# Projecting part of x inside the first ten steps of an attention loop, and reading the output weights in eight parts

## The chip, the cores and the metric

The kernel runs on one core of a Trainium2 chip. The metric is device time in microseconds (us). Before the change the median of three runs is 1559.05 us (1558.44 to 1567.2).

A core has five engines that run side by side, each through its own list of instructions in order: PE (TensorE: matrix multiplies and transposes into PSUM), DVE (VectorE: elementwise work and reductions), ACT (ScalarE: activations and copies), POOL (GpSimd) and SP (SyncE, which here only issues DMAs). They wait for each other on semaphores. DMA transfers are moved by 16 DMA engines that all issuing queues share.

## The reference

One transformer block with adaptive layer norm: 2048 tokens of width D = 640, H = 32 heads of 128 with cached keys and values of 2048 positions, then a small shift mixer and an MLP.

```python
x = A_x
mod = (silu(c) @ w_mod).reshape(1, 6, 1, 640)
sa, ca, ga, sb, cb, gb = (mod[:, i] for i in range(6))
h = layernorm(x) * (1 + ca) + sa
q = (h @ wq) split into 32 heads of 128
p = softmax(q @ k_cache^T * 128 ** -0.5)
x = x + ga * ((p @ v_cache), heads side by side) @ wo
h = layernorm(x) * (1 + cb) + sb
x = x + gb * mixer_and_mlp(h, w1, w2, w3, w4)
```

## The kernel before

**Planning.** The code isn't a list of instructions per engine; it calls `G.op(engine, fn, r=..., w=...)` and `G.dma(...)` with the keys that an operation reads and writes. `Prog` (line 20) derives the semaphore waits from the keys, and each engine runs its operations in the order of these calls. So where a call stands decides what it is behind on its engine. DMAs on "sync" stand in SP's queue in the same way.

**Prologue (lines 329 to 445).** SP issues, in this order: x block 0 (512 rows, 640 KB), c, x block 1, the first third of w_mod (1600 KB, the columns for sa and ca), x blocks 2 and 3, wq and the transposed K and V of head 0, the rest of w_mod (3200 KB), wq and K of head 1, and the whole of wo (5120 KB, line 353). c is turned to columns by its DMA and goes through Silu (363, 364); `cols` (371) multiplies it with w_mod, and ACT writes shift and 1 + scale to mcol (430, 431). Each block cc of x is then taken through four functions: `stats` (bn_stats and bn_aggr on DVE, 384 and 387, and a Sqrt on ACT, 389), `normed` (reciprocal, 393, and (x - mean) * rstd, 396, on DVE), `to_hT` (for each of KT = 5 column blocks: four PE transposes, 407, and an eviction that applies shift and scale, three on ACT, 411, and two on DVE, 416), and `q_head0` (five matmuls with head 0's wq, 250, and an ACT copy to QT, 257). All four blocks are done, but for the last `q_head0`, before the loop. The prologue's scratch (x, w_mod, statistics, the identity) lies in `ring`, the buffer that the loop uses for probabilities.

**Loop (line 558).** A step s handles one tile of 128 queries of one head: 16 tiles a head, NG = 512 in all. PE multiplies Q with K (`qk`, lines 301 and 15) into PSUM in two halves; DVE scales and negates each half into negS and takes its minimum (604); POOL joins the two minima (609); ACT takes the exponential of the 2048 columns to bf16 in Pb (612). The probabilities have to be transposed for the product with V. For tiles 3 and 10 of even heads and 2, 3 and 10 of odd ones (PE_STEPS) PE does it (267) and ACT copies (274); for all others SP issues a DMA transpose from Pb to PTs, mostly two tiles at once (235). `pv` (317) multiplies with V nine steps later (PVD = 9); ring has RP = 10 slots. ACT copies the result to Of every second tile (591), POOL normalizes it (461 to 468) and sends it to DRAM (475). Between these, PE projects the queries of the next head piece by piece (`q_piece`), and SP reads the next wq, K and V.

Steps 0 to 2 also hold `mod_rows` (447): for the other four parts of the modulation, broadcast to all partitions, 25 matmuls and 5 ACT copies (456); step 3 adds 1 to one part (566). Step 0 holds the last `q_head0`. wo is first used when the output projection begins (546), behind the loop.

**Behind the loop** come the output projection, the second layer norm, the mixer and the MLP (lines 642 to 886).

Of the kernel before, what the change touches and what calls it, by code (L numbers as in the profile page):

```python
# [7 lines left out]
ACT = mybir.ActivationFunctionType  # L8
BF16 = mybir.dt.bfloat16
F32 = mybir.dt.float32  # L10
# [113 lines left out]
def bass_adaLN_cond__mha_block_cached__mixer_s_mlp__prompt_kernel(  # L124
# [21 lines left out]
    with ExitStack() as es:  # L146
# [9 lines left out]
        if True:  # L156
            with ExitStack() as es1:
# [32 lines left out]
                XO = SK  # L190
                x_sb = flat[:, XO:XO + NQT * D].rearrange("p (t d) -> p t d", t=NQT)
                WO_ = 6 * SK
                wmod = flat[:, WO_:WO_ + KT * 2 * D].rearrange("p (k n) -> p k n", k=KT)
                RO = 13 * SK
                wmodr = flat[:, RO:RO + KT * 4 * D].rearrange("p (k n) -> p k n", k=KT)
                BO = RO + KT * 4 * D
                s_bc = flat[:, BO:BO + KT * 128].rearrange("p (k q) -> p k q", k=KT)
                ones_f = flat[:, BO + KT * 128:BO + KT * 128 + 256].bitcast(F32)
                SO = BO + KT * 128 + 256
                st = flat[:, SO:SO + NQT * 24].bitcast(F32).rearrange("p (t z) -> p t z", t=NQT)  # L200
                CO = SO + NQT * 24
                c_f = flat[:, CO:CO + 2 * KT].bitcast(F32)
                mcol = flat[:, CO + 2 * KT:CO + 6 * KT].bitcast(F32)
                c_sb = flat[:, CO + 6 * KT:CO + 7 * KT]
                s_col = flat[:, CO + 7 * KT:CO + 8 * KT]
                IO = CO + 8 * KT
                ident = flat[:, IO:IO + 128]
                assert IO + 128 <= 2 * RP * SK and XO + NQT * D <= WO_ and WO_ + KT * 2 * D <= 10 * SK
# [115 lines left out]
                WMK = ringk(WO_, WO_ + KT * 2 * D)  # L324
                WRK = ringk(RO, 2 * RP * SK)
                XK = [ringk(XO + cc * 4 * D, XO + (cc + 1) * 4 * D) for cc in range(NQC)]

                def load_x(cc):
                    G.dma("sync", lambda e: e.dma_start(
                        x_sb[:, 4 * cc:4 * cc + 4], x2d[cc * 512:(cc + 1) * 512, :].rearrange("(t p) d -> p t d", p=128)),  # L330
                        ("x", cc), w=[("x", cc)])

                def load_mod(part, dst, n0, n1):
                    G.dma("sync", lambda e: e.dma_start(
                        dst, w_mod[:, n0:n1].rearrange("(k p) n -> p k n", p=128)), ("wm", part), w=[("wm", part)])

                def load_c(e):
                    with nc.allow_non_contiguous_dma(reason="tiny c vector"):
                        return e.dma_start(c_sb, c[0].rearrange("(kt p) -> p kt", p=128))
# [15 lines left out]
                G.op("gpsimd", lambda g: g.memset(ident, 0.0), w=["id0"])  # L355
                G.op("gpsimd", lambda g: g.memset(ones_f, 1.0), w=["onesf"])
                G.op("gpsimd", lambda g: g.affine_select(out=ident, in_=ident, pattern=[[-1, 128]],
                                                         compare_op=ALU.not_equal, fill=1.0, base=0, channel_multiplier=1),
                     r=["id0"], w=["ident"])
                G.op("gpsimd", lambda g: g.tensor_copy(identf[:], ident), r=["ident"] + ringk(IO, IO + 128), w=["identf"])  # L360
                G.op("gpsimd", lambda g: g.memset(Vaug[:, :, :, 1:2], 1.0), w=["ones"])
                G.op("gpsimd", lambda g: g.memset(Vaug[:, :, :, 258:259], 1.0), w=["ones1"])
                G.op("scalar", lambda a: a.activation(s_col, c_sb, ACT.Silu), r=["c"], w=["scol"])
                G.op("scalar", lambda a: a.activation(c_f, c_sb, ACT.Silu), r=["c"], w=["cf"])
                for k in range(KT):
                    G.op("gpsimd", lambda g, k=k: g.tensor_scalar(out=s_bc[:, k, :], in0=ones_f, scalar1=c_f[:, k:k + 1],
                                                                  scalar2=1.0, op0=ALU.mult, op1=ALU.mult),
                         r=["onesf", "cf"] + WRK, w=[("sbc", k)])

                def cols(t):  # L370
# [7 lines left out]
                    PTp[:, b * 1024:b * 1024 + 512] for b in range(2)]  # L378
                TK = [("Sb", 0), ("Sb", 1), ("Sb", 2), ("Sb", 3), ("O", 0), ("O", 1)]

                def stats(cc):
                    for t in range(4 * cc, 4 * cc + 4):
                        for z in range(2):
                            G.op("vector", lambda v, t=t, z=z: v.bn_stats(st[:, t, 6 * z:6 * z + 6], x_sb[:, t, z * HD:(z + 1) * HD]),  # L384
                                 r=[("x", cc)], w=[("st", t, z)])
                    for t in range(4 * cc, 4 * cc + 4):
                        G.op("vector", lambda v, t=t: v.bn_aggr(mv[:, t, :], st[:, t, :]),
                             r=[("st", t, 0), ("st", t, 1)] + WRK, w=[("mv", t)])
# [526 lines left out]
```

## Time and profile before

| what | value |
|---|---|
| median of 3 runs | 1559.05 us |
| profiled execution's own time | 1558.54 us |
| its span | 1556.4 us |
| granted clock of TensorE, mean | 0.997 |
| PE, DVE, ACT, POOL busy | 94%, 88%, 81%, 42% of the span |
| first L604 (DVE, tile 0) | 36.16 us |
| first exponential (ACT, tile 0) | 39.78 us |
| exponential of tile 10 | 66.56 us |
| last exponential | 1238.0 us |

Times in the profile count from the span's start. Rows of the timeline give start, time taken, engine, line and operation, with the idle time before it and what ended it in brackets. Several instructions in one row are merged. SP's rows are DMA issues: their time is what SP needed to hand the transfer over, not the transfer. A row of waits reads "who waited <- for whom: us in total, times, longest". A row of the windows table gives a stretch, its length, each engine's busy time with its number of instructions, the granted clock, the mean share of the 16 DMA engines (over 1 when packets overlap on an engine) and the rate moved.

### The profile page before, as it was taken

The numbers are of one execution on the slowest core, as the hardware profiler recorded it, in microseconds if no ns is written. First come the engines' busy times: TensorE is split into PE (matmuls) and PEld (weight loads), VectorE is DVE, ScalarE is ACT, GpSimd is POOL, SyncE is SP. The second block draws the span as 40 slices with busy tenths as digits, with TensorE's granted clock in tenths as the row PEclk, the third lists the DMA queues.
The fourth block names the chain that finished last, engine by engine and source line by source line (L and its number), as shares of the span: only waits on it lengthen the run. The fifth ranks groups of instructions, "written<-read, shape, count | busy, mean of one in ns | idle before, by whom it ended". The sixth has DMA issues, their size and how long they took to land.

```text
span 1556.4 us, 32631 instructions
## 1 busy us (share of the span) xinstructions
PE 1463.7 (94%) x13446; PEld 899.4 (58%) x12663; DVE 1375.9 (88%) x2431; ACT 1259.2 (81%) x1177; POOL 647.4 (42%) x1526
## 2 busy tenths in 40 slices
PE   4899999998999999999999999999999899999999
PEld 2466556565656665656566656666565665554545
DVE  6999999999999999999999999999999737667425
ACT  4999999999999999999999999999999800034230
POOL 0145444444445444445444545444454533323100
PEclk9999999999999999999999999999999999999999
DMA  9999999999999999999999999999999998825100
GB/s 300 235 218 227 243 232 229 235 236 239 233 241 239 233 240 234 242 235 226 248 234 240 236 233 244 245 238 226 235 243 234 239 251 184 156 56 140 35 22 35
DMA packets 1123416, 330.32 MB, mean 212 GB/s; under 512 B 1071104, under 2 KB 1117248, under 8 KB 1123264
## 3 DMA queue, kind: packets, MB, share of 16 engines
q1 hardware_dynamic: 1114784, 307.10, 98.6%
q0 software_dynamic: 6144, 16.79, 3.7%
q10 hardware_dynamic: 2336, 4.34, 0.8%
q8 instruction: 104, 1.70, 0.4%
q14 instruction: 48, 0.39, 0.1%
HBM read 43.48 MB, written 19.40 MB: 40 GB/s over the span
## 4 chain that ended last, share of the span: by engine, by line
ACT 54%; PE 21%; DMA 11%; DVE 10%; issue 3%; POOL 1%; SPq 0%; DVEq 0%
ACT ring L612 44%; DMA ring<-ring 10%; PE Sps L546 9%; DVE negS L604 8%; PE Sps L852 4%; ACT ring L274 3%; ACT kv L257 3%; ACT Of L591 3%; PE Oaug L803 2%; PE QPp L803 2%; PE PTp L317 1%; PE Sps L788 1%; DVE ring L384 1%; DMA kv<-Of 0%; PE Oaug L725 0%
## 5 line engine op out<-in xcount | busy, mean ns | idle before, releaser
L604 DVE TENSOR_SCALAR_CACHE_REDUCE negS<-Sps 128x1024 f32<-128x1024 f32 x1024 | 1176.1, 1221 | 26.7 <-PE Sps L15 26.1
L612 ACT ACTIVATE ring<-negS,small 128x2048 bf16<-128x2048 f32 x512 | 1034.9, 2054 | 15.5 <-POOL small L609 14.5
L317 PEld LDWEIGHTS PTp<-kv,ring 128*128 128x128 bf16 x8192 | 546.9, 97 | 351.2 <-issue 89.5
L317 PE MATMUL PTp<-kv,ring 128*128 128x129 bf16 x8192 | 636.4, 221 | 40.5 <-DMA ring<-ring 39.6
L15 PE MATMUL Sps<-kv 128*128 128x512 bf16 x1009 | 382.7, 379 | 9.9 <-DVE negS L604 5.9
L609 POOL TENSOR_SCALAR small<-small 128x1 f32<-128x1 f32 x512 | 145.8, 285 | 574.0 <-DVE negS L604 573.8
L301 PE MATMUL Sps<-kv 128*128 128x512 bf16 x955 | 367.9, 385 | 14.8 <-DVE negS L604 4.4
L468 POOL TENSOR_SCALAR On<-Of,small 128x128 bf16<-128x128 f32 x512 | 190.0, 372 | 13.0
L301 PEld LDWEIGHTS Sps<-kv 128*128 128x128 bf16 x1024 | 98.4, 96 | 127.4 <-DVE negS L604 98.9
L463 POOL TENSOR_TENSOR small<-small 128x4 f32<-128x4 f32 x128 | 133.2, 1041 | 10.0
L475 POOL DMA_DIRECT2D o_scratch<-On x128 | 103.4, 808 | 40.8 <-POOL On L468 37.2
L591 ACT COPY Of<-PTp 128x260 f32<-128x260 f32 x256 | 104.7, 409 | 17.0 <-PE PTp L317 17.0
L250 PE MATMUL Oaug<-hTx,kv 128*128 128x512 bf16 x258 | 97.7, 383 | 4.8 <-DVE hTx L416 4.8
L250 PE MATMUL QPp<-hTx,kv 128*128 128x512 bf16 x259 | 96.8, 378 | 3.2 <-ACT hTx L411 2.5
L733 ACT ACT_TABLE_LOAD x1 | 1.3, 1283 | 111.8 <-POOL hTx L751 111.8
L604 DVE DVE_READ_ACCUMULATOR negS<-Sps 128x1 f32 x1024 | 85.9, 84 | 0.0
L646 POOL TENSOR_SCALAR negS<-negS 128x1 f32<-128x1 f32 x48 | 24.4, 509 | 123.6 <-DVE negS L655 123.6
L546 PE MATMUL Sps<-wo,negS 128*128 128x128 bf16 (+1 forms) x503 | 69.9, 298 | 0.5
L546 PE MATMUL Sps<-wo,hTx 128*128 128x512 bf16 (+1 forms) x502 | 69.4, 298 | 0.5
L660 DVE TENSOR_TENSOR ring<-Sps,mod_bc 128x640 f32<-128x640 f32 x16 | 13.1, 821 | 59.0 <-PE Sps L546 59.0
L856 DVE TENSOR_TENSOR ring<-Sps,ring 128x640 f32<-128x640 f32 x15 | 12.4, 824 | 59.6 <-PE Sps L852 59.6
L267 PE MATMUL QPp<-identf,ring 128*128 128x128 f32 x320 | 61.9, 275 | 0.0
(90 smaller groups left out, 1055.9 us busy)
## 6 DMA issues: line engine op xcount, KB each, us to landing
kv<-in_A_v_cache_dram SPq DMA_DIRECT2D x32, 512.0 KB, 5.1
o_scratch<-On POOLq DMA_DIRECT2D x128, 128.0 KB, 5.0
kv<-in_A_wq_dram SPq DMA_DIRECT2D x32, 160.0 KB, 3.3
wo<-in_A_wo_dram SPq DMA_DIRECT2D x1, 5120.0 KB, 16.6
ring<-ring SPq DMA_TRANSPOSE x240, 7.2
ring<-in_A_x_dram SPq DMA_DIRECT2D x5, 640.0 KB, 7.2
ring<-in_w_mod_dram SPq DMA_DIRECT2D x1, 3200.0 KB, 13.0
out_dram<-wo SPq DMA_DIRECT2D x15, 160.0 KB, 1.8
```

Of the source, the lines that this page charges most:

```text
L15: return t.add_instruction(mybir.InstMatmult(name=t.bass.get_next_instruction_name(), ins=[t.lower_ap(rhs), t.lower_ap(lhsT)], outs=[t.low ...
L250: G.op("tensor", lambda t: t.matmul(JB[jb], wq[:, hb, q, :], hT[:, q, cc * 512:(cc + 1) * 512], start=(q == 0), stop=(q == KT - 1)), r=[(" ...
L301: ins = (t.matmul if c2 == 0 else partial(same_weights, t))(Sps[:, col:col + 512], QT[:, hb, j * 128:(j + 1) * 128], KTs[:, hb, col:col + ...
L317: ins = t.matmul(ob[:, half:half + 129], pt, Vaug[:, hb, c_, v0:v0 + 129], start=(kt == 0), stop=(kt == NKT - 1), skip_group_check=True)
L463: G.op("gpsimd", lambda g: g.tensor_tensor(out=rl[:, 4 * b:4 * b + 4], in0=rl[:, 4 * b:4 * b + 4], in1=mone, op=ALU.pow), r=["mone", ("rl" ...
L468: G.op("gpsimd", lambda g: g.tensor_scalar(out=On[:, b, z, :], in0=Of[:, 2 * b + z // 2, z % 2, 1:129], scalar1=rl[:, 4 * b + z:4 * b + z ...
L475: G.dma("gpsimd", lambda e: e.dma_start(o_scr[jj // 2:jj // 2 + 2, :, hh].rearrange("a p z d -> p a (z d)"), On[:, b].rearrange("p (a z) d ...
L546: ins = t.matmul(YB[b][:, c0:c0 + cw], OTj[pr % 2][:, 2 * hh + z, :], wo[:, hh, c0:c0 + cw], start=(hh == 0), stop=(hh == H - 1))
L591: G.op("scalar", lambda a, p=p: a.copy(Of[:, p % 4].rearrange("p z d -> p (z d)"), PO[:, (p % 2) * 512:(p % 2) * 512 + 260]), r=[("O", p % ...
L604: G.op("vector", lambda v, half=half, dst=dst, src=src, r8=r8: v.tensor_scalar(out=dst, in0=src, scalar1=-SCALE, scalar2=None, op0=ALU.mul ...
L609: G.op("gpsimd", lambda g, r8=r8: g.tensor_scalar(out=nm[:, r8:r8 + 1], in0=nm0[:, r8:r8 + 1], scalar1=nm1[:, r8:r8 + 1], scalar2=None, op ...
L612: G.op("scalar", lambda a, s=s, r8=r8: a.activation(Pb[:, s % RP, :], negS[:, s % 3, :], ACT.Exp, bias=nm[:, r8:r8 + 1], scale=-1.0), r=[( ...
```

## The change

Four edits.

1. The prologue's scratch for w_mod's second part, statistics, small vectors and identity moves from `ring` to the buffer of wo (`wof`); x and w_mod's first part stay in the first ten slots of ring. The key "WOR" is read by all that use this scratch and written by the first part of wo.
2. DMA order: x block 0, w_mod's first part, x block 1, wq and K of head 0, x blocks 2 and 3, wq of head 1, w_mod's second part, V of head 0, K of head 1. c goes as rows on ACT's queue and is turned by a matmul with the identity. wo is read in eight parts of four heads (640 KB) from SP's queue, at steps 13, 15, 17, 20, 23, 27, 30 and 33.
3. Before the loop: block 0 as a whole, statistics and normalization of block 1, and half of block 2's statistics. `bn_stats` of blocks 1 to 3 are called in halves. A dummy Exp stands behind the last Sqrt. The rest is called from tables: `EARLY` after the step's matmuls and ahead of its exponential, `LATE` after its exponential. The evictions of blocks 1 to 3 are all on ACT (in block 0 two of five are on DVE), and the roots of blocks 2 and 3 are a power on POOL.
4. `mod_rows` goes from steps 0 to 2 to steps 3, 4, 5 and 7, with one PSUM bank of its own choice for each call.

```diff
-                RO = 13 * SK
-                wmodr = flat[:, RO:RO + KT * 4 * D].rearrange("p (k n) -> p k n", k=KT)
+                wof = wo[:].rearrange("p h n -> p (h n)")
+                wmod = flat[:, 0:KT * 2 * D].rearrange("p (k n) -> p k n", k=KT)
+                XO = [4 * SK, 4 * SK + 4 * D, 7 * SK, 7 * SK + 4 * D]
+                wmodr = wof[:, 0:KT * 4 * D].rearrange("p (k n) -> p k n", k=KT)
...
+                WOP = H // 8
+
+                def load_wo(i):
+                    G.dma("sync", lambda e: e.dma_start(
+                        wo[:, i * WOP:(i + 1) * WOP], A_wo[i * WOP * 128:(i + 1) * WOP * 128, :].rearrange("(h p) n -> p h n", p=128)),
+                        ("wo", i), w=(["WOR"] if i == 0 else []) + [("wop", i)] + (["wo", "woz", "wo4"] if i == 7 else []))
+                G.dma("scalar", lambda e: e.dma_start(c_row, c[0].rearrange("(kt p) -> kt p", p=128)), "c", r=WOR, w=["c"])
                 load_x(0)
-                G.dma("sync", load_c, "c", w=["c"])
+                load_mod(0, wmod, 0, 2 * D)
                 load_x(1)
-                load_mod(0, wmod, 0, 2 * D)
+                load_wq(0)
+                load_k(0)
                 for cc in range(2, NQC):
                     load_x(cc)
-                load_wq(0)
-                load_k(0)
-                load_v(0)
-                load_mod(1, wmodr, 2 * D, 6 * D)
                 if H > 1:
                     load_wq(1)
+                load_mod(1, wmodr, 2 * D, 6 * D)
+                load_v(0)
+                if H > 1:
                     load_k(1)
-                G.dma("sync", lambda e: e.dma_start(wo[:], A_wo.rearrange("(h p) n -> p h n", p=128)), "wo", w=["wo", "woz", "wo4"])
...
+                G.op("tensor", lambda t: t.matmul(JB[0][:, 0:KT], c_row, ident[0:KT, 0:KT], start=True, stop=True),
+                     r=["c", "ident"] + WOR, w=[("J", 0)])
...
+                def root(cc, on_act):
+                    c4 = slice(4 * cc, 4 * cc + 4)
+                    if on_act:
+                        G.op("scalar", lambda a: a.activation(sd[:, c4], mv[:, c4, 1], ACT.Sqrt, bias=float(EPS)),
+                             r=[("mv", t) for t in range(4 * cc, 4 * cc + 4)], w=[("sd", cc)])
+                        G.op("vector", lambda v: v.reciprocal(rstd[:, c4], sd[:, c4]), r=[("sd", cc)], w=[("rstd", cc)])
+                    else:
+                        G.op("gpsimd", lambda g: g.tensor_scalar(out=sd[:, c4], in0=mv[:, c4, 1], scalar1=float(EPS),
+                                                                 scalar2=1.0, op0=ALU.add, op1=ALU.mult),
+                             r=[("mv", t) for t in range(4 * cc, 4 * cc + 4)], w=[("sd", cc)])
+                        G.op("gpsimd", lambda g: g.tensor_tensor(out=rstd[:, c4], in0=sd[:, c4], in1=mh4, op=ALU.pow),
+                             r=[("sd", cc), "mh4"] + WOR, w=[("rstd", cc)])
...
+                def to_hT(cc, ks, banks, on_v=()):
+                    for k, b in zip(ks, banks):
+                        turn(cc, k, b)
+                    for k, b in zip(ks, banks):
+                        modul(cc, k, b, k in on_v)
...
-                stats(0)
-                normed(0)
-                stats(1)
+                stats(0, 0, 4)
+                root(0, True)
+                normed(0)
+                stats(1, 0, 2)
                 G.op("tensor", cols, r=["scol", ("wm", 0)] + WMK + WOR, w=[("J", 1)])
...
-                normed(1)
-                to_hT(0)
-                for cc in range(NQC):
-                    if cc + 2 < NQC:
-                        stats(cc + 2)
-                        normed(cc + 2)
-                    if cc + 1 < NQC:
-                        q_head0(cc)
-                        to_hT(cc + 1)
+                to_hT(0, range(KT), range(KT), (1, 3))
+                stats(1, 2, 4)
+                q_head0(0)
+                root(1, True)
+                G.op("scalar", lambda a: a.activation(dume, mh4[:, 0:1], ACT.Exp), r=["mh4"] + WOR, w=["dume"])
+                normed(1)
+                stats(2, 0, 2)
+                bcast()
+                EARLY = {0: [(to_hT, 1, (0, 1, 2), (4, 5, 7), ())],
+                         1: [(to_hT, 1, (3, 4), (4, 5), ())],
+                         2: [(to_hT, 2, (0, 1), (4, 5), ()), (q_head0, 1)],
+                         3: [(to_hT, 2, (2, 3), (4, 5), ()), (mod_rows, 0, 2)],
+                         4: [(to_hT, 2, (4,), (4,), ()), (mod_rows, 1, 1), (mod_rows, 2, 2), (q_head0, 2)],
+                         5: [(to_hT, 3, (0, 1), (4, 5), ()), (mod_rows, 3, 2)],
+                         6: [(to_hT, 3, (2, 3), (4, 5), ())],
+                         7: [(to_hT, 3, (4,), (4,), ()), (mod_rows, 4, 1)],
+                         8: [(mod_end,)],
+                         9: [(q_head0, 3)]}
+                LATE = {0: [(stats, 2, 2, 4), (root, 2, False)],
+                        1: [(normed, 2)],
+                        2: [(stats, 3, 0, 2)],
+                        3: [(stats, 3, 2, 4), (root, 3, False)],
+                        4: [(normed, 3)]}
+                WOAT = {13: [0], 15: [1], 17: [2], 20: [3], 23: [4], 27: [5], 30: [6], 33: [7]}
...
-                    if s <= 2:
-                        for i in ((0,), (1, 2), range(3, len(MROW)))[s]:
-                            mod_rows(i)
...
-                        if s == 0 and half == 1:
-                            q_head0(NQC - 1)
...
                     for fn, x, y in evacs:
                         fn(x, y)
+                    for fn, *args in EARLY.get(s, ()):
+                        fn(*args)
...
                             r=[("negS", s % 3), ("nm", r8)], w=[("Pb", s % RP)])
+                        for fn, *args in LATE.get(s, ()):
+                            fn(*args)
...
                             load_wq(h + 2)
+                        for i in WOAT.get(s, ()):
+                            load_wo(i)
```

`turn` (four PE transposes of one column block) and `modul` (its eviction, with shift and scale) are the two halves of the former `to_hT`; `mod_end` is the former step 3's addition together with the memset of line 443, and `bcast` the former line 366.

More of the change, by code (lines that the diff above doesn't have):

```diff
@@ L334, in load_mod @@
                     G.dma("sync", lambda e: e.dma_start(
[L335 to L339, printed above, removed]
+                        dst, w_mod[:, n0:n1].rearrange("(k p) n -> p k n", p=128)), ("wm", part), r=WOR, w=[("wm", part)])
@@ L454, in f @@
                         return ins
-                    G.op("tensor", f, r=[("sbc", k) for k in range(KT)] + [("wm", 1)] + WRK, w=[("O", i % 2)])
-                    G.op("scalar", lambda a: a.copy(mod_bc[:, n0:n1], bank), r=[("O", i % 2)], w=[("mod", i)])
+                    G.op("tensor", f, r=[("sbc", k) for k in range(KT)] + [("wm", 1)] + WOR, w=[key])
+                    G.op("scalar", lambda a: a.copy(mod_bc[:, n0:n1], bank), r=[key], w=[("mod", i)])
+                mone = small[:, 0:4]
@@ new lines, in bass_adaLN_cond__mha_block_cached__mixer_s_mlp__prompt_kernel, with mod_end @@
+                MROW = [(n0, min(n0 + 512, 4 * D)) for n0 in range(0, 4 * D, 512)]
+                def mod_end():
+                    G.op("gpsimd", lambda g: g.tensor_scalar(
+                        out=mod_bc[:, 2 * D:3 * D], in0=mod_bc[:, 2 * D:3 * D], scalar1=1.0, scalar2=1.0, op0=ALU.add, op1=ALU.mult),
+                        r=[("mod", i) for i in range(len(MROW))], w=["mod"])
+                    G.op("gpsimd", lambda g: g.memset(mone, -1.0), w=["mone"] + [("mv", t) for t in range(NQT)])
@@ L548, in f @@
                         return ins
-                    G.op("tensor", f, r=[("OT", pr % 2, i) for i in parts] + [("OTa", pr % 2)] + ["wo", "woz", "wo4"], w=[("S", b)])
+                    G.op("tensor", f, r=[("OT", pr % 2, i) for i in parts] + [("OTa", pr % 2)] + ["wo", "woz", "wo4"] + [("wop", i) for i in range(8)], w=[("S", b)])
                     return b
```

140 lines of the change are left out of this document (66 added, 74 removed).

## The prediction

> **What bounds the kernel now.** I read the windows table first, then the queue of SP by time, the waits by stretch, and last the first 40 us. In the windows table (window, its length, then each engine's busy time with its count, granted clock, DMA share, GB/s) the loop's engines are all nearly full, so a share alone doesn't name the bound:
>
> ```profile
> 36.00:46.00 10.00, 9.10 (x41) 3.31 (x35) 5.65 (x9) 7.66 (x9) 0.59 (x2) 1.00 1.06 394
> 46.00:56.00 10.00, 6.59 (x27) 1.96 (x19) 10.00 (x19) 8.55 (x7) 1.80 (x5) 1.00 0.77 180
> ...
> 86.00:96.00 10.00, 9.87 (x103) 6.72 (x94) 10.00 (x19) 10.00 (x10) 4.91 (x13) 1.00 1.03 191
> ...
> 300.00:400.00 100.00, 93.62 (x938) 59.25 (x869) 96.87 (x168) 96.93 (x87) 47.02 (x115) 1.00 1.18 234
> ```
>
> VectorE is at 10.00 of 10 until about 150 us, then at 97%. Its spacing per tile while full is 2.29 us; from exponential 3 (50.18) to the last (1238.0, the 512th) it is 1187.8 / 508 = 2.34. Something else takes the difference. The queue of SP by time (start, time taken, line, count) shows it:
>
> ```profile
> 93.87 4.09 SPq L235 DMA_TRANSPOSE ring<-ring  x1
> 98.00 0.58 SPq L222 DMA_DIRECT2D kv<-in_A_wq_dram  x1
> 98.89 11.23 SPq L235 DMA_TRANSPOSE ring<-ring  x2
> 110.17 0.58 SPq L227 DMA_DIRECT2D kv<-in_A_v_cache_dram  x1
> 110.80 21.00 SPq L235 DMA_TRANSPOSE ring<-ring  x5
> 131.84 2.12 SPq L216 DMA_TRANSPOSE kv<-in_A_k_cache_dram  x1
> ```
>
> From 98.9 us each row begins where the one before ended, and so to 1250 us (no gap over 0.45 us). A transpose of two tiles takes SP 3.9 to 4.2 us while the queue is short (45.51, 56.79) and about 4.7 later (four in 18.95 from 149.88), so SP is held back by the engines behind it. The waits, first for 60 to 158 us, where no wait on a DMA is listed, then for 158 to 260 us:
>
> ```profile
> PEld PTp L317 <- DMA ring<-ring: 9.1, 10, 1.5
> ...
> PE PTp L317 <- DMA ring<-ring: 4.3, 7, 1.0
> ...
> DVE negS L604 <- PE Sps L15: 2.3, 5, 0.7
> ```
>
> So the loop is paced by VectorE until the transposes' backlog reaches what PVD = 9 tiles forgive (near 158 us, tile 45 to 47), and by the DMA queue from there on: VectorE loses 2.3, 5.2 and 12.2 us to it in 158 to 260, 260 to 500, 500 to 1240. Since that queue is never empty after 98.9 us, **whatever DMA work is added behind that point moves the end by its full time**, and whatever brings the queue's start forward is kept. What precedes the loop is a chain on VectorE (the chain of waits):
>
> ```profile
> 10.86 3.15 DVE ring L384 x8
> ...
> 17.24 3.15 DVE ring L384 x8
> ...
> 23.62 3.15 DVE ring L384 x8
> ```
>
> Two of these three statistics and their normalizations are what the change moves.
>
> **Step 1, the loop begins earlier.** Up to 10.86 us VectorE's rows stay (x of block 0 lands at 5.0). Then: half of block 1's statistics, (3.23 + 0.41) / 2 = 1.8, to 12.7; two evictions of block 0, 0.99 (L416), to 13.7; the other half, 1.8, to 15.5; root and reciprocal, 0.78 (8.57 to 9.35 before), to 16.3; normalization 1.51, to 17.8; half of block 2's statistics, 1.8, to 19.6. There the first L604 starts, against 36.16. The first exponential follows 2.8 us later as before, without the table load in front of it (1.28, moved under the normalization): 22.4 against 39.78. Cover: w_mod's first part is now second in the queue; 1600 KB at 395 GB/s after 5.0 is 9.2, its 50 matmuls end near 10.7, before the transposes of block 0 (xh at 10.86). x of block 1 comes at 10.9, wq and K at 13 (3 MB after 5.0; at 237 GB/s 17.6, still under 19.6). ScalarE evicts block 0 by 14, the projection and QT end near 15.5. c, now five rows on ScalarE's queue and one matmul, has until 9.2. That leaves 4 us of slack; if K came later than 19, it would be late next.
>
> **Step 2, ScalarE pays in the first ten tiles.** From exponential 0 to exponential 10 its instructions, by their spacing in its own rows, are: 10 exponentials at 1.90 = 19.0; 12 evictions of hT (5 + 5 + 5 less the three ahead of exponential 0) at 0.67 (1.45 for two, less the overlap) = 8.0; 5 copies of mod rows and 3 of head 0's projection at 0.47 = 3.8; and what stood there already, 3 copies of head 1, 2 of transposes at 0.47 and one of Of at 0.25 = 2.6. Sum 33.4, and 1 for late releases (exponentials 1 and 2 wait for VectorE). VectorE over the same tiles: 10 x 2.29 + 1.8 + 1.5 + 3.6 + 1.5 = 31.3, so ScalarE is the longer one and covers it. Exponential 10 at 22.4 + 34.4 = 56.8, against 66.56: **10 us gained of the 17**. Were the two to add instead, 34.4 + 8.4 leaves 1.4; were the copies free, 17.4 stays. I take 10, since neither waits for the other for long: S, negS and the banks give one to three tiles.
>
> Behind it: POOL's roots (0.28 + 1.04 each) end a microsecond before the next L609 that queues behind them; mod_end (0.72) waits for the last copy in step 7 and is done just before exponential 8 is due. PE gets 60 transposes and 25 + 15 matmuls into steps it was idle in (6.59 of 10 in 46 to 56); mod rows need w_mod's second part, 3200 KB, near 27 us, asked for near 34. SP's transposes queue behind K of head 1, as before; they have room, since a tile now takes 3.4 us.
>
> **Step 3, wo.** Before, 5120 KB moved from 33 to 47.5 us, with nothing behind it: SP's next transpose came at 45.5. Its rate there, while it had the engines alone (window, length, clock, share, GB/s):
>
> ```profile
> 38.00:41.00 3.00, 1.00 1.06 395
> 41.00:44.00 3.00, 1.00 1.06 396
> 59.00:62.00 3.00, 1.00 1.17 265
> ```
>
> At 395 GB/s the 5.24 MB are 13.3 us of all 16 engines. In tiles 13 to 33 they stand between transposes (the third row has transposes nearly alone: 265). No row shows wo in that company: the low end is SP's issue alone, 8 x 0.58 = 4.6; the high end the loop's mean rate, 237 GB/s, 22.1 us. I take 14, by the nearest row, the same bytes alone, and a little for sharing.
>
> The Trainium skill, "DMA: Bandwidth & Descriptors", section "Measured (HBM→SBUF, 128 partitions, SWDGE, issued from GpSimd)", has a rule against the split: transfers under 1 MiB lose efficiency, and 1 MB gets 341 GB/s. By that the eight 640 KB parts would take at least 15.4 us (an estimate), and the sum below would be 1561.8. The trace of SP's transfers disagrees: 8 to 11 us moved 416 GB/s with parts of 640 and 1600 KB.
>
> **Step 4, what the queue did not use.** In before SP had 2.1 us of gaps between tile 13's transpose (75.55) and 98.9 us (1.76 at 92.1, 0.31 at 98.6). wo fills them, so 2.1 of its price is free. The first part also waits for every reader of the scratch that now lies in wo; the last are in steps 8 and 9, four tiles earlier, and were they late, the transposes from tile 14 on would stand behind it in SP's queue. The rest of the price makes the backlog reach its limit near tile 25 in place of 45.
>
> **Sum**, against the profiled execution, 1558.54 us (span 1556.4 and 2.1 around it, 0.5 under the median 1559.05): -10 - 2.1 + 14 = +1.9, so **1560.4**.
>
> **Rivals.** *wo is hidden.* If the engines can take large packets between the transposes' small ones, only issue time or nothing is paid: -10 + 0 to 2.5, 1549 to 1551. For it: no wait on a DMA before 158 us. Against: 1.18 of share and SP's rows end to end; two transposes cost 4.7 in place of 4.1 when others share. *wo at the loop's rate*, the side of slower: 22.1 in tiles 13 to 33, -10 - 2.1 + 22.1 = +10, 1568.5; slower than before from a price of 12.1 us on, which is near my value. For it: the 4.7 just named. Against: the 395. *Table loads.* Evictions of hT (Identity) come between exponentials in steps 0 to 7. If each group brought two loads of 1.28, ScalarE has 20.5 more, exponential 10 comes at 77.3: +10.7 - 2.1 + 14 = +22.6, 1581. Against: casts and copies stand between exponentials with one load in 512, and Identity ran under the root's table without its own. The Trainium skill, "ScalarE: Activation LUTs", section "Table sets: the hidden batching unit", has identity in every set, which would exclude it. *The loop does not begin earlier*, because K or w_mod comes late: then 0 - 2.1 + 14 = +11.9, 1570; the bytes speak against it.
>
> **Numbers.** Forecast 0.60, wo hidden 0.16, wo at the loop's rate 0.16, table loads 0.04, no earlier start 0.04. The range 1548 to 1571 takes the first three with the ends of wo's price and leaves out the table loads and half the last. One per cent, 15.6 us, is about what a measurement of this kernel tells from no change: only the table loads and the tail of the dear wo lie above it (0.08), and below 1543 only a hidden wo with evictions that cost ScalarE little (0.03). Within: 0.89.
>
> **What would show it.** First L604 near 19.6; exponential 10 near 57; 12 evictions of hT among exponentials and no ACT_TABLE_LOAD between them; eight issues of wo at 0.58 with SP's rows end to end from tile 13; PE's first waits on a DMA near tile 25, some 90 us, not 158; VectorE's waits for PE in the loop up from 19.7 to near 32 us. It is wrong if SP's queue has gaps after tile 33 (then the queue is no bound and the gain stays), or if tile 10 is under 5 us earlier.

## The result, and the profile after

The changed kernel takes 1567.44 us (median of 14 runs, 1563.75 to 1571.97), the kernel before in the same comparison 1558.74 (14 runs, 1554.89 to 1567.2). The ratio is **1.0051, 95% interval 1.0034 to 1.0068**: 8.7 us slower, and within the one per cent that was forecast. The forecast was 1560.4, that is +1.9 on the execution it was made against; the profiled execution after is 1567.99 (span 1566.1), which is +9.5 on that one.

One thing about the changed kernel has to be known before it is copied: it reads head 2's projection weights at step 6 into the buffer from which `q_head0` still projects the last 512 queries of head 0 at step 9, so these queries are projected with head 2's weights. e8, e9 and e10 below read them at step 9 instead, and e9 shows no change of the time by it.

The loop does begin earlier. VectorE's rows of the timeline after (start, time taken, engine, line, operation, operands, count): two halves of statistics of block 1, half of block 2, then the first maximum of tile 0.

```profile
10.70 1.67 DVE L395 BATCH_NORM_STATS2 wo<-ring 128x6 f32<-128x320 bf16 x4
...
13.41 1.66 DVE L395 BATCH_NORM_STATS2 wo<-ring 128x6 f32<-128x320 bf16 x4
...
17.56 1.66 DVE L395 BATCH_NORM_STATS2 wo<-ring 128x6 f32<-128x320 bf16 x4
...
19.38 1.17 DVE L644 TENSOR_SCALAR_CACHE_REDUCE negS<-Sps 128x1024 f32<-128x1024 f32 x1
```

Against 36.16 that is 16.8 us earlier. ScalarE's rows of the same timeline show where half of it goes: five copies and evictions stand between exponentials 3 and 4 (L652), which are 4.64 us apart instead of the 1.90 of exponentials end to end. No load of a table is among them.

```profile
35.26 2.03 ACT L652 ACTIVATE ring<-negS,small 128x2048 bf16<-128x2048 f32 x1
37.16 0.60 ACT L260 CAST kv<-QPp 128x512 bf16<-128x512 f32 x1
37.63 0.82 ACT L430 ACTIVATE hTx<-PTp,wo 128x512 bf16<-128x512 bf16 x1
38.30 0.62 ACT L461 COPY mod_bc<-PTp 128x512 f32<-128x512 f32 x1
38.77 0.64 ACT L461 COPY mod_bc<-Oaug 128x512 f32<-128x512 f32 x1
39.41 0.58 ACT L260 CAST kv<-QPp 128x512 bf16<-128x512 f32 x1
39.90 2.00 ACT L652 ACTIVATE ring<-negS,small 128x2048 bf16<-128x2048 f32 x1
```

The windows table after (window, length, busy time of PE, its weight loads, VectorE, ScalarE and POOL with counts, granted clock, DMA share, GB/s) answers to the one shown of before:

```profile
36.00:46.00 10.00, 8.37 (x55) 4.01 (x48) 8.75 (x19) 9.99 (x13) 1.94 (x4) 1.00 0.08 19
46.00:56.00 10.00, 9.18 (x66) 4.60 (x62) 8.39 (x15) 10.00 (x11) 1.87 (x6) 1.00 0.78 177
86.00:96.00 10.00, 9.46 (x98) 5.94 (x90) 9.88 (x19) 10.00 (x9) 4.56 (x11) 1.00 1.09 258
...
126.00:136.00 10.00, 5.21 (x46) 3.42 (x42) 5.03 (x10) 6.67 (x6) 3.34 (x8) 0.77 1.23 259
300.00:400.00 100.00, 93.66 (x930) 59.48 (x862) 97.60 (x171) 98.89 (x90) 49.25 (x119) 1.00 1.21 236
```

Read its last two columns first. In 36 to 46 us before moved 394 GB/s, and that was wo; now the DMA engines stand idle there (share 0.08). In 126 to 136 VectorE was full before, as this row of before shows:

```profile
126.00:136.00 10.00, 9.61 (x100) 6.40 (x91) 10.00 (x19) 10.00 (x12) 5.10 (x13) 1.00 1.21 229
```

Now it is busy there for 5.03 of 10, while the DMA share is 1.23: the queue holds the loop up. SP's queue by time shows what is in it. A transpose of two tiles, 4.1 to 4.7 before, takes SP 6.4 to 7.1 where it stands behind a part of wo (behind the last part 4.8), and the rows follow each other without a gap:

```profile
70.87 0.58 SPq L343 DMA_DIRECT2D wo<-in_A_wo_dram  x1
71.50 6.38 SPq L238 DMA_TRANSPOSE ring<-ring  x1
77.92 0.58 SPq L343 DMA_DIRECT2D wo<-in_A_wo_dram  x1
78.55 7.07 SPq L238 DMA_TRANSPOSE ring<-ring  x1
85.66 0.58 SPq L343 DMA_DIRECT2D wo<-in_A_wo_dram  x1
86.29 4.46 SPq L219 DMA_TRANSPOSE kv<-in_A_k_cache_dram  x1
```

The waits after, from 60 to 160 us ("who waited <- for whom: us in total, times, longest"; PEld is PE loading weights), where before had not one wait on a transpose until 158:

```profile
PEld PTp L320 <- DMA ring<-ring: 16.2, 7, 5.1
DVE negS L644 <- PE Sps L15: 15.5, 7, 5.3
...
PE PTp L320 <- DMA ring<-ring: 12.1, 5, 4.6
```

VectorE loses 15.5 us there. In 160 to 260, 260 to 500 and 500 to 1250 it loses 1.5, 6.2 and 13.1, together 20.8, against 19.7 before: the rest of the loop is as it was.

### The profile page after: what moved, and what is told of

It is laid out like the page before. It is cut to its first block, busy times and chain, and to the rows that moved or that the text cites. A ratio compares the mean times of both kernels' runs of the same rounds, so it can differ in the third digit from the quotient of the medians.

```text
span 1566.1 us, 32640 instructions
## 1 busy us (share of the span) xinstructions
PE 1470.1 (94%) x13447; PEld 902.0 (58%) x12664; DVE 1373.1 (88%) x2423; ACT 1263.7 (81%) x1182; POOL 650.6 (42%) x1531
## 4 chain that ended last, share of the span: by engine, by line
ACT 52%; PE 20%; DMA 16%; DVE 8%; issue 3%; POOL 1%; SPq 0%; DVEq 0%
ACT ring L652 43%; DMA ring<-ring 14%; PE Sps L593 7%; DVE negS L644 7%; PE Sps L896 4%; ACT ring L277 3%; ACT kv L260 3%; ACT Of L629 3%; PE QPp L847 2%; PE Oaug L847 2%; PE PTp L320 2%; DMA negS<-o_scratch 1%; PE Sps L832 1%; DMA ring<-in_A_x_dram 1%; DMA kv<-Of 1%
## 5 line engine op out<-in xcount | busy, mean ns | idle before, releaser
L652 ACT ACTIVATE ring<-negS,small 128x2048 bf16<-128x2048 f32 x512 | 1031.5, 2046 | 20.2 <-POOL small L649 19.0
L629 ACT COPY Of<-PTp 128x260 f32<-128x260 f32 x256 | 102.5, 400 | 17.1 <-PE PTp L320 17.0
L704 DVE TENSOR_TENSOR ring<-Sps,mod_bc 128x640 f32<-128x640 f32 x16 | 13.1, 821 | 57.8 <-PE Sps L593 33.8
L270 PE MATMUL Oaug<-identf,ring 128*128 128x128 f32 x320 | 61.9, 275 | 1.6 <-ACT mod_bc L461 1.6
```

The lines of the kernel that those rows point to most:

```text
L629: G.op("scalar", lambda a, p=p: a.copy(Of[:, p % 4].rearrange("p z d -> p (z d)"), PO[:, (p % 2) * 512:(p % 2) * 512 + 260]), r=[("O", p % ...
L652: G.op("scalar", lambda a, s=s, r8=r8: a.activation(Pb[:, s % RP, :], negS[:, s % 3, :], ACT.Exp, bias=nm[:, r8:r8 + 1], scale=-1.0), r=[( ...
```

## The experiments

They ran on three chips, where the kernel before takes 1546.55 (A: e1 to e4), 1545.56 (B) and 1545.95 us (C), some 13 us less than where the result was taken; its runs there spread over 20 us (1535 to 1556). The times that e1 to e4 expect count from the 1558.7 and 1567.4 of the first comparison, so read them as differences. Times are compared as ratios to before on the same chip, and the price of wo is read in the traces by a measure that is free of what comes later: **the time from exponential 16 to exponential 64**. At VectorE's 2.29 us a tile it is 109.9. The columns that give a time of an exponential, or "16 to 64", are read from one traced execution each.

| kernel | chip | median us | ratio to before, 95% | exp 16 at | 16 to 64 | last exp at |
|---|---|---|---|---|---|---|
| before (first trace) | – | 1558.74 | – | 80.20 | 111.30 | 1238.01 |
| after | – | 1567.44 | 1.0051 (1.0034–1.0068) | 71.28 | 127.62 | 1245.56 |
| c_before | B | one run, 1556.63 | – | 79.50 | 110.87 | 1236.57 |
| b2_before | C | 1546.86 | 0.9996 (0.9957–1.0034) | 79.85 | 110.82 | 1234.89 |
| c_after | B | 1557.19 | 1.0085 (1.0052–1.0118) | 69.73 | 127.18 | 1234.93 |
| e2, before with wo in parts | A | 1573.73 | 1.0184 (1.0153–1.0214) | 79.45 | 128.41 | 1253.18 |
| e1, wo at tile 3 | A | 1544.15 | 0.9991 (0.9963–1.0019) | 73.72 | 110.85 | 1222.76 |
| e8, the same mended | B | 1541.96 | 0.9985 (0.9955–1.0016) | 70.25 | 111.30 | 1223.88 |
| e10, the same, one transfer | C | 1542.89 | 0.9974 (0.9948–1.0001) | 71.27 | 110.90 | 1221.62 |
| e5, wo whole at tile 13 | B | 1551.53 | 1.0053 (1.0025–1.0081) | 70.09 | 122.08 | 1229.88 |
| e7, parts from ScalarE's queue | C | 1558.68 | 1.0054 (1.0022–1.0087) | 70.34 | 126.25 | 1238.05 |
| e9, head 2's weights at tile 9 | C | 1562.41 | 1.0092 (1.0056–1.0129) | 70.16 | 128.78 | 1244.24 |
| e3, wo spread | A | 1557.79 | 1.0082 (1.0054–1.0110) | 69.85 | 110.86 | 1234.50 |
| e4, wo read twice | A | 1583.03 | 1.0242 (1.0208–1.0276) | 70.07 | 127.93 | 1262.49 |

My theory: the DMA queue is full behind tile 13, so wo costs what it adds to the queue, wherever in the full queue it stands, and nothing in a stretch where the queue is empty. Rivals: the loss is in the ten early steps (ScalarE's copies, a wait for weights), or in the order in SP's queue, or in the split into parts.

**The two halves of the change apart.** e2 is before with the eight parts alone:

```diff
-                G.dma("sync", lambda e: e.dma_start(wo[:], A_wo.rearrange(...)), "wo", w=["wo", "woz", "wo4"])
...
+                WOAT = {13: [0], 15: [1], 17: [2], 20: [3], 23: [4], 27: [5], 30: [6], 33: [7]}
...
+                        for i in WOAT.get(s, ()):
+                            load_wo(i)
```

> The kernel before with one part of the change alone: wo in eight parts at tiles 13 to 33, the rest as it was. Queue theory: 18.3 us for wo less the 2.1 us in which SP's queue stood open before 99 us, 1558.7 + 16.2 = 1575 (1572 to 1578), with tile 10 still at 66.6 us. Rival (the projections cost, wo does not): 1558 to 1561.

From exponential 16 to 64 it takes 128.41, 17.1 to 17.6 more than the three traces of before. Its waits from 60 to 170 us are those of after:

```profile
PEld PTp L317 <- DMA ring<-ring: 20.8, 8, 5.7
DVE negS L610 <- PE Sps L15: 16.9, 9, 6.0
```

So the loss needs nothing of the early start. By the medians it is 27 us (1.53 to 2.14%), more than the forecast 16 and than the trace's 17; that surplus is taken up below.

e1 keeps the early start and puts wo where the engines are idle, at tile 3; the second part of w_mod goes back into free slots of the ring, so that the first seven parts of wo are free to be written.

```diff
-                wmodr = wof[:, 0:KT * 4 * D].rearrange("p (k n) -> p k n", k=KT)
+                wmodr = flat[:, RO:RO + KT * 4 * D].rearrange("p (k n) -> p k n", k=KT)
...
-                WOAT = {13: [0], 15: [1], 17: [2], 20: [3], 23: [4], 27: [5], 30: [6], 33: [7]}
+                WOAT = {3: range(7), 8: [7]}
```

> The changed kernel, but seven of the eight parts of wo are read at tile 3 and the last at tile 8, in the 10 us in which the changed kernel's DMA queue is empty (35 to 46 us); to make room the scratch for w_mod's second part goes back to ring and the small scratch lies in wo's last two heads, and the last mod row moves from step 7 to step 5. Queue theory (in the loop DMA time is conserved, and wo between the transposes costs 18 us): only the early start is left, 8.9 us under the kernel before at tile 10 and kept to the end, about 1549 (1547 to 1552). Rival (the loss comes from the projections in the loop, not from wo): it stays near 1567.

By the medians it is 2.4 us faster than before, and the interval holds no change, where some 10 us were expected. In its trace wo's price is gone (110.85), but the start lost 2.4 to 4 us of its gain (exponential 16 at 73.72, after's at 71.28 and 69.73): a row of the modulation waited for an eviction of the same bank, and head 0's last projection waited 2.7 us for weights that now queue behind wo. e8 mends both:

```diff
-                         5: [(to_hT, 3, (0, 1), (4, 5), ()), (mod_rows, 3, 2)],
+                         5: [(to_hT, 3, (0, 1), (4, 5), ()), (mod_rows, 3, 2), (mod_rows, 4, 3)],
...
-                         7: [(to_hT, 3, (4,), (4,), ()), (mod_rows, 4, 1)],
+                         7: [(to_hT, 3, (4,), (4,), ())],
...
-                        if j == 6 and h + 2 < H:
+                        if j == (9 if h == 0 else 6) and h + 2 < H:
```

> As the first experiment (wo at tiles 3 and 8), mended in two places that cost it 6.5 us of VectorE's time between 40 and 57 us: the last mod row takes a bank that no eviction waits in, and wq of head 2 is asked for at step 9, behind the last projection of head 0. In the changed kernel it is asked for at step 6 and replaces head 0's weights ahead of that projection, so the last 512 queries of head 0 are projected with head 2's weights; this kernel projects them with head 0's. Queue theory: tile 16's exponential near 71, as in the changed kernel, 8 us ahead of the kernel before, and the end 8 to 10 us under it. Rival (a gain ahead of the loop is lost in it): the end within 3 us of the kernel before, as in the first experiment.

Exponential 64 comes at 181.55 us, 8.8 to 10 earlier than in the three traces of before, and 15.4 to 17.4 earlier than in the two of after. Against after on the same chip that is 1541.96 to 1557.19, **15.2 us less**, and the two differ in wo's place, in the scratch that makes room for it, and in the two mends. So in the traces the early start itself works, and in after its gain is spent on wo. Against before the medians show only 3.6 us (the interval holds no change), where 8 to 10 were expected; by them alone the rival of this expectation, an end within 3 us of before, is not excluded.

**Is it the split?** e5 reads wo in one transfer of 5120 KB at tile 13:

```diff
-                        wo[:, i * WOP:(i + 1) * WOP], A_wo[i * WOP * 128:(i + 1) * WOP * 128, :].rearrange(...)),
+                        wo[:], A_wo.rearrange("(h p) n -> p h n", p=128)),
...
-                WOAT = {13: [0], 15: [1], 17: [2], 20: [3], 23: [4], 27: [5], 30: [6], 33: [7]}
+                WOAT = {13: [0]}
```

> The changed kernel with wo as one transfer of 5120 KB at tile 13 in place of eight. Queue theory: the same bytes between the same transposes, so the end is that of the changed kernel within 2 us, though all of the stall comes at once near tiles 14 to 24. By the page's rule on transfers under 1 MiB it would be 2 us or more faster. Rival (the eight places matter): 5 us or more to either side.

It misses "within 2 us": 1551.53 against 1557.19 on the same chip, and 122.08 against 127.18 in the traces. SP's queue in e5 has the two transposes behind wo at 23.43 us, and its windows show why: the engines move 394 to 396 GB/s, wo's rate alone, while PE runs out of work.

```profile
69.79 0.58 SPq L343 DMA_DIRECT2D wo<-in_A_wo_dram  x1
70.42 23.43 SPq L238 DMA_TRANSPOSE ring<-ring  x2
93.89 2.38 SPq L219 DMA_TRANSPOSE kv<-in_A_k_cache_dram  x1
```

```profile
75.00:80.00 5.00, 4.92 (x50) 3.08 (x44) 5.00 (x11) 5.00 (x5) 1.64 (x5) 1.00 1.06 396
80.00:85.00 5.00, 2.46 (x25) 1.60 (x22) 4.31 (x8) 5.00 (x6) 2.93 (x7) 1.00 1.06 394
85.00:90.00 5.00, 0.00 (x0) 0.00 (x0) 0.00 (x0) 1.39 (x1) 0.00 (x0) 0.71 1.23 277
90.00:100.00 10.00, 8.30 (x59) 5.54 (x56) 4.53 (x7) 3.78 (x5) 1.24 (x4) 0.63 1.16 244
```

One stall of 9.5 us takes the place of seven, and the price is 122.08 - 111.0 = 11.1 (111.0 is the mean of the three traces of before), where the eight parts cost 16.2 and 16.6 in the two traces of after (17.4 in e2, 17.8 in e9). With the 2.1 us of gaps in SP's queue that wo fills, e5's wo takes 13.2 us, near the 13.3 of the same bytes alone.

Does the split cost by itself, or only among transposes? e10 is e8 with its first seven parts as one transfer of 4480 KB:

```diff
+                    i0, i1 = (0, 7) if i == 0 else (7, 8)
-                        wo[:, i * WOP:(i + 1) * WOP], A_wo[i * WOP * 128:(i + 1) * WOP * 128, :].rearrange(...)),
+                        wo[:, i0 * WOP:i1 * WOP], A_wo[i0 * WOP * 128:i1 * WOP * 128, :].rearrange(...)),
...
-                WOAT = {3: range(7), 8: [7]}
+                WOAT = {3: [0], 8: [7]}
```

> The mended version with wo at tile 3 (1.0, 1542.0 us there, 0.9985 of before), with one more edit: the first seven parts are one transfer of 4480 KB and not seven of 640 KB. It tells whether the 5.7 us that the whole transfer saved at tile 13 are a property of the split, or of what stands between the parts. If large transfers move better by themselves, some 5 us come back here too: 1536 to 1538, ratio 0.995. If the split costs only where transposes stand between the parts, it is the same here, since the seven parts are issued back to back: ratio 0.997 to 1.000.

Its windows while wo moves:

```profile
40.00:43.00 3.00, 3.00 (x21) 1.38 (x18) 2.09 (x4) 3.00 (x4) 0.29 (x1) 1.00 1.06 390
43.00:46.00 3.00, 2.50 (x20) 1.48 (x17) 2.68 (x5) 3.00 (x5) 0.12 (x1) 1.00 1.06 396
46.00:49.00 3.00, 2.42 (x14) 0.85 (x10) 3.00 (x5) 3.00 (x4) 0.91 (x3) 1.00 1.06 394
```

The seven parts of e8, back to back, moved 387, 392 and 385 GB/s in the same windows. The ratios are 0.9974 and 0.9985, each inside the other's interval; that interval is too wide to exclude the 0.995 of the other expectation, but the rates, at most 3% apart, leave no 5 us in a transfer of 12. So parts of 640 KB cost next to nothing by themselves. That they cost 5 us because transposes stand between them is argued from this: no run puts eight parts back to back at tile 13.

These two runs also give a second count of the price, since SP's queue has no gap and no wo in it from the issue of tile 13's transpose to that of tiles 64 and 65. The stretch takes 121.5 us in e8 and 121.3 in e10, 134.7 in e5, and 141.1 and 140.7 in after and c_after: 13.2 to 13.4 us for wo in one transfer again, and 19.2 to 19.7 for the eight parts.

**Is it the order in SP's queue?** e7 issues the parts from ScalarE's queue, past the transposes:

```diff
-                    G.dma("sync", lambda e: e.dma_start(
+                    G.dma("scalar", lambda e: e.dma_start(
```

> The changed kernel with one edit: the eight parts of wo are issued by ScalarE's queue and not by SP's, at the same tiles. If wo's price is its share of the 16 DMA engines, the bytes cost the same wherever they are issued: within 3 us of the changed kernel (1.0085 of before, 1557.2, on the second chip of the experiments). If the price is the order in SP's queue (a transpose that stands behind a part of wo), then parts on another queue pass beside the transposes and 5 us or more come back: 1552 or less, as one whole transfer gave (1.0053, 1551.5). Against a gain: each issue takes ScalarE some 0.6 us, 5 us for eight, where ScalarE has no slack until tile 16.

126.25, a price of 15.3: the bytes cost nearly the same. Four transposes at 60.82 now take SP 28.18 us with no part of wo among them in its queue, and the waits from 60 to 160 us stand as in after:

```profile
60.82 28.18 SPq L238 DMA_TRANSPOSE ring<-ring  x4
```

```profile
DVE negS L644 <- PE Sps L15: 14.7, 8, 5.8
PEld PTp L320 <- DMA ring<-ring: 13.6, 4, 5.5
```

So the price of the parts does not need SP's order; what the two queues have in common is the 16 engines. In the medians (1.0054, with 1.0092 for e9 on the same chip) the intervals overlap, and nothing follows from them.

**Place and amount.** e3 spreads the parts, one in every third head; e4 reads wo a second time, at tiles 61 to 81.

```diff
-                WOAT = {13: [0], 15: [1], 17: [2], 20: [3], 23: [4], 27: [5], 30: [6], 33: [7]}
+                WOAT = {13: [0], 61: [1], 109: [2], 157: [3], 205: [4], 253: [5], 301: [6], 349: [7]}
```

> The changed kernel with the eight parts three heads apart, at tiles 13, 61, 109, 157, 205, 253, 301 and 349. Queue theory: the queue is never empty in the loop, so each part costs its 2.3 us wherever it stands; 1566 to 1569, with no crowd of waits near 100 to 140 us. Rival (the price is that of crowding eight parts into 20 tiles; one part in three heads is taken up by the nine tiles of lead): only the early start is left, 1549 to 1555.

```diff
...
-                WOAT = {13: [0], 15: [1], 17: [2], 20: [3], 23: [4], 27: [5], 30: [6], 33: [7]}
+                WOAT = {13: [0], 15: [1], 17: [2], 20: [3], 23: [4], 27: [5], 30: [6], 33: [7],
+                        61: [0], 63: [1], 65: [2], 68: [3], 71: [4], 75: [5], 78: [6], 81: [7]}
```

> The changed kernel that reads wo twice, the second time at tiles 61 to 81 into the same place. Queue theory: no gap is left to fill there, so the second reading shows the whole price, 18.3 us: 1567.4 + 18.3 = 1586 (1584 to 1588). By wo's rate alone on the engines (395 GB/s) it would be 13.3, 1581; by the loop's mean rate (237 GB/s) 22, 1589.5. Rival (the loop absorbs it when the queue has its backlog already): under 1572.

Spread out, one part lies before tile 61 and costs nothing that shows (110.86), but the end is where it is in after: 1.0082 against 1.0085 and 1.0051. From exponential 64 to the last it takes 1053.8 us, 7 to 16 more than after and c_after (1046.7, 1038.0). Twice, the second reading costs 20.3 to 22.7 us from exponential 64 to 128 (170.75 against 150.46 and 148.09), and 25.8 by the medians (1583.03 - 1557.2, by c_after on another chip), more than the 18.3 expected. Its waits from 198 to 369 us:

```profile
PEld PTp L320 <- DMA ring<-ring: 29.4, 15, 6.0
DVE negS L645 <- PE Sps L15: 23.1, 11, 6.2
```

Both fit a full queue in which place doesn't matter, though for e3 the evidence is thin: single executions of one kernel differ by about as much (8.6 us between after and c_after). The second reading has no gap and no lead left to use, and pays about the loop's mean rate, the 22.1 of my high end.

**The early steps.** e9 is after with head 2's weights loaded at tile 9, after the last use of head 0's in that buffer:

```diff
-                        if j == 6 and h + 2 < H:
+                        if j == (9 if h == 0 else 6) and h + 2 < H:
```

> The changed kernel with one edit: head 2's projection weights are loaded at tile 9 and not at tile 6, after the last use of head 0's in the same buffer. In the changed kernel the last 512 queries of head 0 are projected with head 2's weights, and that projection waits for their transfer. Only the wait of PE for it (2.7 us in the profile of after, near tile 9) can come back: 0 to 2 us faster than the changed kernel, since the tiles have a lead there. If it were 4 us or more, the gain of 8.9 us in the first ten tiles that I read in the trace would be limited by this wait and not by ScalarE's added copies.

No gain: 1.0092, in the interval of c_after's 1.0085, and exponential 16 comes at 70.16 (c_after 69.73). The wait for these weights cost nothing that shows; ScalarE, busy for 9.99 and 10.00 of 10 us from 36 to 56, is left as what sets the ten tiles.

**What the comparison itself gives.** Two of the kernels are before and after unchanged.

> The kernel before itself, for its profile on the chip of this group, since its time there differs from that of the first runs (1546.6 against 1558.7). Queue theory: where it is faster, VectorE waits less for PE in the loop than the 19.7 us of the first profile (each us less there is a us of time), and PE's waits for DMA begin later than 158 us. Rival: the difference lies ahead of or behind the loop.

> The changed kernel itself, in one group with the experiments. Queue theory: early start 8.9 less, wo 18.3 more, less what the kernel before leaves open in its queue on this chip (2.1 on the first one). If that is again 2.1: +7.3, ratio 1.005. If the kernel before keeps its queue open longer here, wo costs the same but more of it was free: +4 to +7. Rival (a loop that is filled doesn't return to its rate): over +12.

> The kernel before once more, unchanged, against itself. It shows what the comparison gives for no change at all, and how far the times of before differ within one chip. On the first chip its runs had a median of 1558.7 us, on the two chips of the experiments 1545.6 and 1546.6, with runs from 1536 to 1554, while its one profiled run there took 1556.6. If the chips differ, profiled and timed runs agree here and the ratio is 1.000, with an interval of about 0.003 each way. If before has two ways to run (a short backlog in the DMA queue that stays short, and a long one that stays long), its own runs lie in two groups some 10 us or more apart, on one chip.

No change gives 0.9996, and its interval (0.9957 to 1.0034) holds 1, as it should. c_after's +11.6 us lies above the +4 to +7.3 that was expected, just under the rival's +12. But before's own runs reach from 1537 to 1556 without falling into two groups, and after's on chip B from 1554 to 1563. The traces show one thing that differs: the first head that takes longer than VectorE's 36.6 us is that of tiles 48 to 63 in the first trace of before (37.9), that of 64 to 79 in c_before (37.7), and in b2_before those from 48 to 95 still take 36.6 to 36.7. When the queue begins to hold the loop up is a matter of the single execution in before; in after, c_after, e9 and e2 the head from tile 16 on takes 39.7 to 40.9 already. It agrees with that, but doesn't show, that before's medians there lie 11 and 7 us under the runs of its two traces (1556.63 and 1552.91), and that the medians make wo dearer (27 us in e2) and the early start less worth (3.6 in e8) than the traces do. **This stays open**: no trace is kept of a run of before near 1537.

## Why the prediction held, and where it was off

- *What bounds the loop.* Held in the main. SP's rows follow end to end, a second reading and spread parts cost about the full time, wo in an idle stretch costs none that the traces show. But PE's first wait on a transpose in before, at 159.0 us, falls in tile 51 by VectorE's rows, not in 45 to 47; and in b2_before VectorE keeps its rate to tile 95, so even before the queue does not bind from one fixed tile on.
- *Step 1.* Held: first maximum at 19.38 (forecast 19.6), first exponential at 22.77 (22.4).
- *Step 2.* Nearly: exponential 10 at 57.69 for 56.8. From exponential 0 it takes 34.9 where 34.4 were summed; the gain is 8.9, not 10 (9.8 in the traces of chip B: 56.11 and 65.86). No table load came, so that rival fell, and so did the one of no earlier start.
- *Step 3* failed by its size: **wo's price, taken at 14, is 18.3.** In the trace, from the issue of tile 13's transpose to that of tiles 64 and 65, before needs 124.9 us (75.55 to 200.42) and after 141.1 (66.72 to 207.80): 16.2 more, and 2.1 of gaps. The same count on chip B, with 2.85 of gaps, gives 19.9, and against e8 it was 19.2 to 19.7, so 18.3 is the low end. I chose the rate that these bytes have alone. e5 shows that they get it, 13.2 us, but as one transfer; in eight parts among transposes they don't. The rival of the loop's rate, 22.1, was priced too high for the first reading and right for a second (20.3 to 22.7); a price of 12.1 was named as the point from which the change is slower, and it was passed.
- *Step 4.* Held: the first part waited for no late reader, the gaps are filled, and PE first waits for a transpose at 88.9 us, where "some 90" was said. VectorE waits for PE for 36.3 us from 60 us on (15.5 + 1.5 + 6.2 + 13.1), where 32 was said.
- *The sum* is then -8.9 - 2.1 + 18.3 = +7.3, and exponential 64 comes 7.4 us later than before (198.90 and 191.50), the last one 7.5 later. The pair on chip B agrees at exponential 64 (6.5 later), but not at the last, which comes 1.6 us earlier in c_after; so behind exponential 64 one pair of traces shows little. The remaining 1.9 of the profiled +9.5 lies behind the loop, where single executions of one kernel differ as much (315.8 to 318.4 us from the last exponential to the end in the three of before).
- *The number.* The result fell inside the range, but nearer to the rival's 1568.5 than to the forecast's 1560.4. In this pair of traces that is luck: the rival's price was 3.8 us too dear, and a start worth 1.1 us less and 1.9 us behind the loop, which were not forecast, make up for most of it.
- *wo hidden* fell: it would have needed what e8 and e10 do, 10 us of idle engines, which the change itself made at 36 to 46 us and left empty.

The Trainium skill, "DMA: Bandwidth & Descriptors", section "Measured (HBM→SBUF, 128 partitions, SWDGE, issued from GpSimd)", says that transfers under 1 MiB lose efficiency. I set it aside because SP's small transfers moved 416 GB/s alone. By e5 its direction holds inside the loop, and its estimate of 15.4 was nearer than my 14; by e8 and e10, alone, it doesn't (385 to 392 GB/s in parts, 390 to 396 in one).

## What to carry to other kernels

When a transfer is moved, read first what the queue does at its old place and at its new one: here 10 us of idle engines were left behind, and 18 to 20 us of a full queue were paid to start 9 us earlier. A big read belongs into the stretch that the queue does not use, back to back; if it must stand in a full queue, one transfer was 5 us cheaper than eight parts among transposes. For a change of half a per cent, a price read between two fixed tiles of the trace says more than medians that spread over 20 us.

## What was not expected of the hardware

**The granted clock falls where the loop stalls.** In e5, by windows of three microseconds:

```profile
83.00:86.00 3.00, 0.00 (x0) 0.00 (x0) 1.31 (x4) 3.00 (x4) 0.68 (x3) 1.00 1.06 396
86.00:89.00 3.00, 0.00 (x0) 0.00 (x0) 0.00 (x0) 0.39 (x1) 0.00 (x0) 0.69 1.27 235
89.00:92.00 3.00, 0.35 (x4) 0.36 (x5) 0.00 (x0) 0.00 (x0) 0.00 (x0) 0.50 1.24 277
92.00:95.00 3.00, 3.00 (x21) 2.23 (x18) 0.98 (x1) 0.00 (x0) 0.00 (x0) 0.50 1.12 254
95.00:98.00 3.00, 3.00 (x21) 1.75 (x18) 1.54 (x5) 2.49 (x2) 0.62 (x2) 0.60 1.09 201
98.00:101.00 3.00, 2.95 (x32) 1.81 (x28) 3.00 (x5) 2.29 (x3) 1.44 (x3) 1.00 1.23 270
```

PE has nothing from 83 to 89; from 86 on the clock falls, and when work is back at 92 it runs at 0.50, so that VectorE is busy for 0.98 of 3.00 behind a PE that is full. From 98 on it is 1.00 again. A wait for a transfer thus brings some microseconds of slow matmuls with it; after shows the same in 126 to 136 (0.77). The Trainium skill, "TensorE: Matmul & The Clock Gate", section "Part 1: The HAM clock gate (the "warmup" mystery)", states it: an idle window of about 3.4 us halves the clock, and a busy one of the same length restores it; the rows agree. Kernels whose parts stall the loop have a mean clock of 0.990 to 0.995 in their profiled runs (after 0.992), those with wo at tile 3 0.997 to 1.0. These slow stretches alone do not explain the 5 us that the parts cost over one transfer: from exponential 16 to 64 the mean clock is 0.95 in after, 0.96 in e5 and 0.97 in e2, and e2 pays 6 us more than e5. The DMA share over the same tiles is 1.19 in e5, but 1.15 in after and 1.14 in e2. Whether packets of wo and of transposes hinder each other in the engines, or the repeated stalls leave the queue short of work, no run here tells apart.

**One program, 13 us apart.** The kernel before takes 1558.74 us where the result was taken and 1545.6 to 1546.6 on the three chips of the experiments, at nearly the same granted clock (0.997 in the first profiled run, mostly 0.996 to 0.999 there). Which chip the result was taken on is not on record, so that the chip makes the difference is likely, not shown.
